# Second MLP product in three float32r products, interleaved tile by tile with the first

## The chip, the cores and the metric

The kernel runs on one core of a Trainium2 chip. The core has a matrix engine (TensorE, "PE" in the profile, with its weight loads as "PEld"), VectorE (DVE), ScalarE (ACT), GpSimd (POOL) and a queue engine SyncE (SP) that issues most of the DMA transfers. Each engine works off its own instructions in order, and they meet through semaphores. SBUF is the working memory of 128 partitions; PSUM holds TensorE's results in eight banks of 128 x 512 float32. The metric is device time in microseconds (us), the median of the runs. The profile is one more execution, with its own span, from its first to its last instruction.

## The reference

Two stages follow each other. The first is a state-space scan over 4 batches, 8 heads and 768 tokens, 32 channels and 16 states per head. It is computed in pieces of the sequence:

```python
cum = np.cumsum(log_a)                                   # within the piece
M = (C @ B.T) * exp(cum_i - cum_j) * causal
y = M @ x + (C @ state) * exp(cum)
state = exp(sum(log_a)) * state + sum_j exp(cum_end - cum_j) * B_j x_j
```

The second takes the scan's result as 3072 tokens of 256 features:

```python
h = x @ w_in                        # 256 -> 2048
g = h * clip(h + 3, 0, 6) / 6
out = g @ w_out                     # 2048 -> 256
```

The two weight arrays arrive as float64 words (8 bytes each) and are decoded to float32 on the chip.

## The kernel before

The sequence is cut into six blocks of 128 tokens. A block holds these tokens of all four batches, so 512 columns. For each block k the scan produces yT (features by tokens, two tiles of 128 x 512), the first product makes the hidden tile h for each of 16 groups f of 128 hidden units, an activation turns it into gT, and the second product sums over the 16 groups. The program is written in the order in which each engine runs it (a manual schedule); nothing reorders it.

*Head and block 0.* The scan of block 0 is done first. Then `mlp_in` runs the first product of block 0 in plain float32, while the weights, in eight pieces of 1 MB, are loaded into `raw` (three buffers) and decoded: `decode` is a generator of steps on ScalarE and VectorE (L206 to L254), and steps of the next pieces are woven between the groups of block 0. `split_w` splits each piece of `w_in` into a high part, a low part and a combination called gap. `first_out` (L735) is the second product of block 0, in float32 with the tokens as output rows, and is stored by two plain DMAs.

*Blocks 1 to 5, first product.* `lead` (L684 through `in_product`) multiplies the gap parts of weight and y, and the result is scaled in PSUM (L697 on VectorE or L700 on ScalarE). `follow` adds high times high and low times low on top. These three float32r products give the full float32 product. ScalarE (L707) and VectorE (L708) then make gT. Six PSUM banks rotate for h, and `lead` runs two groups ahead.

*Blocks 1 to 5, second product.* It starts when the block's gT is complete. It is one level of a Strassen-Winograd scheme in float32: seven products in place of eight, on quarters of gT and w_out. The sums of weights (`weight_sums`) are made once, the sums of gT (`g_sums`, L780) by GpSimd in each block. For blocks 1 to 4 `wide_units` (L861) keeps the output features on partitions and the tokens in columns; the result is transposed in 32 x 32 squares on VectorE (L875) and stored by 32 DMAs of 16 KB (L882). The last block uses `out_units` (L794): tokens on partitions, and four plain stores (L847).

*The scan of the next block* (`scores`, `multiply`, `mix`, `from_state`, `renew`: L548, L589, L615, L521, L560) is put between the products of `wide_units`, all eight heads at once. The decay factors are loaded as rows, masked by GpSimd (`conceal`, L162) and exponentiated by ScalarE, one call of 128 x 64 per batch and head with the column's own sum as bias (`decay`, L406, 32 calls per block). The loads of the coming blocks, `load_bc`, `load_x` and `rows`, are issued by SP in program order with the stores.

Of the kernel before, what the change touches and what calls it, by code (L numbers as in the profile page):

```python
# [21 lines left out]
def kernel(  # L22
# [12 lines left out]

    nc = tc.nc
# [22 lines left out]
    ffn = ctx.enter_context(tc.tile_pool(name="ffn", bufs=1))  # L70
    ps = ctx.enter_context(tc.tile_pool(name="ps", bufs=1, space=PSUM))
    ps_o = ctx.enter_context(tc.tile_pool(name="ps_o", bufs=2, space=PSUM))
    ps_y = ctx.enter_context(tc.tile_pool(name="ps_y", bufs=1, space=PSUM))
    dram = ctx.enter_context(tc.tile_pool(name="dram", bufs=1, space=DRAM))
    ctx.enter_context(tc.manual_schedule())


    pre = ffn.tile([P, NF, TB], FP32, name="pre", tag="gT")
    G = NB * NH


    moe_w_in, moe_w_out = moe_w_in.bitcast(U32), moe_w_out.bitcast(U32)
    a_sb = pre[:G, 0:2].rearrange("g t i -> g (t i)")[:, :S]
# [5 lines left out]
    def load_bc(c):  # L89


# [19 lines left out]
        Bs[c] = tokens_first(B, nc.scalar if c == 0 else nc.sync, name="B")  # L111
# [7 lines left out]
    def load_x(c):  # L119
# [4 lines left out]
    w_high, w_low, w_gap = (  # L124
        const.tile([P, NK, DF], FP32R, name=n) for n in ("w_high", "w_low", "w_gap"))
    w_out = const.tile([P, NF, DM], FP32, name="w_out")
# [4 lines left out]

    def load_w(i, queue=nc.sync):

# [12 lines left out]
    load_w(0, nc.scalar)  # L146
    load_bc(0)
    load_x(0)
    load_w(1)
    nc.scalar.preload_act_table_set("natural_log_exp_and_others")  # L150


# [16 lines left out]
    run = pre[:G, 2:4].rearrange("g t i -> g (t i)")[:, :S]  # L169
# [7 lines left out]
    half_up = const.tile([P, 1], FP32, name="half_up")  # L177
    nc.vector.memset(half_up, UP / 2)
# [14 lines left out]
    first_in = {}  # L193

    def decode(i):

# [33 lines left out]
        if i and i + NRAW < 2 * NP:  # L233
            load_w(i + NRAW)
# [3 lines left out]
        if i < NP:  # L238
            if i < 2:
                dst = ffn.tile([P, NK, FP * P], FP32, name="w32", tag=("wide", "back")[i])  # L240
                first_in[i] = [dst[:, j] for j in range(NK)]
                m, e = (t.rearrange("p (k f) -> p k f", k=NK) for t in (m, e))
            else:
                first_in[i] = [y_tile("w32", FP32) for j in range(NK)]
                for j, dst in enumerate(first_in[i]):
                    sl = slice(j * FP * P, (j + 1) * FP * P)
                    nc.vector.scalar_tensor_tensor(  # L247
                        out=dst, in0=m[:, sl], scalar=2.0 ** -20, in1=e[:, sl], op0=ALU.mult,
                        op1=ALU.mult)
                return  # L250
        else:
            dst = w_out[:, (i - NP) * FP:(i - NP + 1) * FP, :]
            m, e = (t.rearrange("p (k f) -> p k f", k=FP) for t in (m, e))
        nc.vector.scalar_tensor_tensor(  # L254
            out=dst, in0=m, scalar=2.0 ** -20, in1=e, op0=ALU.mult, op1=ALU.mult)

    pick = const.tile([P, G], BF16, name="pick")  # L260
    less = const.tile([P, G], BF16, name="less")
    picks = ffn.tile([P, G * N], BF16, name="picks", tag="u2")
    mid = pre[:G, 9].bitcast(BF16)[:, :2 * P]
    low = pre[:G, 10, :2 * P]

    cum = pre[:G, 4:6].rearrange("g t i -> g (t i)")[:, :S]
# [74 lines left out]
    def y_tile(name, dtype):  # L341
        return att.tile([P, TB], dtype, name=name, tag="y", bufs=6)

    yTs, states, mids, bTs, bss, tmps = {}, {}, {}, {}, {}, {}
    ys, cbs, sps, adds = {}, {}, {}, {}

    ds = {}

    def diff_mask(c, b):

        if c == 0:
            d = ps.tile([P, NH, HT], FP32, name="d", tag=f"f{b}")
        elif b < 2:
            d = ps_o.tile([P, NH, HT], FP32, name="d", tag="o")
        else:
            d = ps_y.tile([P, NH, HT], FP32, name="d", tag=f"y{b % 2}")
        nc.tensor.matmul(
            out=d, lhsT=ident_h, rhs=hide.unsqueeze(1).to_broadcast([P, NH, HT]),
            start=True, stop=True)
        ds[c, b] = d  # L360

    def mask_again(c, b):

        nc.tensor.matmul(
            out=ds[c, b], lhsT=ident_h, rhs=hide.unsqueeze(1).to_broadcast([P, NH, HT]),
            start=True, stop=True)
# [21 lines left out]
    def first_eto():  # L388

        e_ps = ps.tile([P, NB, HT], FP32, name="e_ps", tag="f0")  # L390
# [10 lines left out]

    def decay(c, b):

        for h in range(NH):
            g = b * NH + h
            nc.scalar.activation(  # L406
                Ls[c][:, b, h], Ls[c][:, b, h], AF.Exp, bias=cum_n[:, c, g:g + 1])
# [5 lines left out]

# [8 lines left out]

# [12 lines left out]
    def turn_ps(c, j):  # L435

        if c < 2:
            return ps.tile([P, NB, P], FP32, name="t_ps", tag=f"f{2 * j if c else 1}")
        return ps_o.tile([P, NB, P], FP32, name="t_ps", tag="o")

# [7 lines left out]
    def turn_b(c):  # L448

        t_ps = turn_ps(c, 1)  # L450
        transposes(c, 1, t_ps)
        nc.scalar.copy(out=turned(c)[0], in_=t_ps)

    def turn_c(c, t_ps):

        transposes(c, 0, t_ps)
# [10 lines left out]

        nc.vector.tensor_tensor(out=turned(c)[2], in0=t_ps, in1=etos[c], op=ALU.mult)

    def turn(c, j):  # L470
        if j:
            turn_b(c)
        else:
            t_ps = turn_ps(c, 0)
            turn_c(c, t_ps)
            fade_c(c, t_ps)

    def wake(c):
        from_start(c)
        carry(c)  # L480
        for b in range(NB):
            ends(c, b)

    def turn_squares(t, out):

# [15 lines left out]
    def turn_all(c):  # L501
        bT, _, csT = turned(c)
        for t, out_ in zip(bcs[c], (csT, bT)):
            turn_squares(t, out_)
        part_heads(c)
        fade(c)
# [636 lines left out]
```

## Time and profile before

| | us |
|---|---|
| runs | 362.24, 359.21, 362.02 |
| median | 362.02 |
| profiled execution, span | 356.9 |
| TensorE busy | 337.6 (95%) |
| VectorE busy | 223.0 (62%) |
| ScalarE busy | 183.1 (51%) |
| GpSimd busy | 165.1 (46%) |
| mean granted TensorE clock | 0.999 |

The profile states its execution's span, 356.9 us; what lies around the span is not in it, and the runs are 2.3 to 5.3 us above it. A busy share is the sum of an engine's instructions over the span. TensorE's instructions overlap, so the spacing of a run of matmuls says more than their duration. A float32 matmul appears as two records, a float32r matmul as one. A line such as "150.09 21.50 PE h L684 x92" of the chain of work reads: from 150.09 us on, for 21.50 us, 92 records of line 684 that write h. A window's line gives its bounds and length, then for PE, PEld, DVE, ACT and POOL the busy time and the number of records, then the granted clock, the DMA share and GB/s.

### The profile page before, as it was taken

How to read it: one execution, taken by the hardware profiler on the slowest of the kernel's cores; microseconds unless marked ns; L12 is line 12 of the kernel's file. 1: busy time of each engine (PE TensorE's matmuls, PEld its weight loads, DVE VectorE, ACT ScalarE, POOL GpSimd, SP SyncE). 2: the span in 40 equal slices, each digit the busy share in tenths (PEclk: the TensorE clock that was granted, in tenths of full speed). 3: DMA queues.
4: the chain of work that ended last, by engine and by line, in shares of the span. 5: the costliest groups of instructions: out<-in, count | busy, mean ns of one | idle time of the engine just before them, and what ended most of it. 6: DMA issues, size and time to landing. Idle time of an engine off the chain costs nothing.

```text
span 356.9 us, 8261 instructions
## 1 busy us (share of the span) xinstructions
PE 337.6 (95%) x3408; PEld 266.9 (75%) x3408; DVE 223.0 (62%) x341; ACT 183.1 (51%) x380; POOL 165.1 (46%) x155
## 2 busy tenths in 40 slices
PE   6999768899799999999999999999999989999996
PEld 2654225688687888888888887888888778888996
DVE  6689999976567654967345777327677313577011
ACT  3779678655876375166293266292466021466000
POOL 3304667075139981239931259911079600079600
PEclk9999999999999999999999999999999999999999
DMA  7989637800693007524106624106110001110000
GB/s 168 204 330 153 151 118 158 165 2 3 92 194 57 17 3 119 109 35 66 30 2 105 125 34 66 31 2 77 24 21 2 2 2 17 28 18 0 2 29 29
DMA packets 91604, 24.88 MB, mean 70 GB/s; under 512 B 84208, under 2 KB 87952, under 8 KB 91056
## 3 DMA queue, kind: packets, MB, share of 16 engines
q1 hardware_dynamic: 87184, 23.06, 33.3%
q10 hardware_dynamic: 4384, 1.31, 1.6%
q8 instruction: 26, 0.43, 0.5%
q14 instruction: 10, 0.08, 0.1%
HBM read 21.07 MB, written 3.29 MB: 68 GB/s over the span
## 4 chain that ended last, share of the span: by engine, by line
PE 77%; DVE 14%; ACT 3%; DMA 3%; issue 1%; SPq 1%; DVEq 0%
PE h L684 31%; PE wb L861 12%; PE wc L861 8%; PE wa L861 8%; PE o L735 4%; PE oa L794 4%; PE ob L794 4%; DVE gT L720 3%; PE y L615 2%; PE y L521 2%; DVE w L247 2%; PE cb L548 2%; DMA raw<-in_moe_w_in_dram 2%; ACT L L406 2%; DVE wse L225 2%
## 5 line engine op out<-in xcount | busy, mean ns | idle before, releaser
L708 DVE SCALAR_TENSOR_TENSOR gT<-gT,h 128x512 f32<-128x512 f32 x80 | 55.0, 688 | 33.5 <-ACT gT L707 30.5
L707 ACT ACTIVATE gT<-h,half_up 128x512 f32<-128x512 f32 x80 | 55.2, 690 | 36.2 <-PE h L684 36.2
L780 POOL TENSOR_TENSOR s<-gT 128x512 f32<-128x512 f32 x20 | 25.8, 1290 | 66.4 <-DVE gT L708 66.4
L684 PE MATMUL h<-gap,w_gap 128*128 128x512 f32 x160 | 51.7, 408 | 2.0 <-DVE gap L677 2.0
L684 PE MATMUL h<-high,w_high 128*128 128x512 f32 x160 | 50.7, 398 | 0.3 <-DVE h L697 0.3
L684 PE MATMUL h<-low,w_low 128*128 128x512 f32 x160 | 50.3, 395 | 0.0
L700 ACT ACTIVATE h<-h 128x512 f32<-128x512 f32 x40 | 23.6, 589 | 30.2 <-PE h L684 30.2
L684 PEld LDWEIGHTS h<-gap,w_gap 128*128 128x128 f32 x160 | 29.9, 188 | 9.2 <-ACT high L675 1.6
L684 PEld LDWEIGHTS h<-high,w_high 128*128 128x128 f32 x160 | 29.6, 188 | 8.6 <-DVE h L697 1.8
L684 PEld LDWEIGHTS h<-low,w_low 128*128 128x128 f32 x160 | 30.1, 188 | 7.3
L641 PE MATMUL h<-yT,w 128*128 128x512 f32 x64 | 29.3, 603 | 4.8 <-DVE w L247 2.4
L735 PE MATMUL o<-w_out,gT 128*128 128x256 f32 x128 | 29.0, 382 | 3.0 <-DVE w_out L254 3.0
L406 ACT ACTIVATE L<-L,cum_n 128x64 f32<-128x64 f32 x128 | 31.4, 337 | 0.0
L861 PE MATMUL wb<-s,w_out 128*128 128x256 f32 x128 | 30.7, 382 | 0.0
L589 DVE TENSOR_TENSOR L<-L,cb 128x512 f32<-128x512 f32 x24 | 15.3, 681 | 22.8 <-PE cb L548 19.7
L735 PEld LDWEIGHTS o<-w_out,gT 128*128 128x128 f32 x128 | 23.9, 190 | 7.4 <-ACT gT L715 2.3
L697 DVE TENSOR_SCALAR h<-h 128x512 f32<-128x512 f32 x40 | 27.7, 692 | 1.2 <-PE h L684 1.2
L641 PEld LDWEIGHTS h<-yT,w 128*128 128x128 f32 x64 | 11.6, 189 | 21.8 <-issue 10.4
L780 POOL TENSOR_TENSOR gT<-gT 128x512 f32<-128x512 f32 x20 | 26.7, 1337 | 0.0
L861 PEld LDWEIGHTS wb<-s,w_out 128*128 128x128 f32 x128 | 24.0, 190 | 3.5
L162 POOL TENSOR_SCALAR_AFFINE_SELECT L<-L 64x1024 f32<-64x1024 f32 (+1 forms) x16 | 18.6, 1166 | 17.3 <-DMA L<-cum_d 17.0
L780 POOL TENSOR_TENSOR s<-s,gT 128x512 f32<-128x512 f32 x20 | 25.7, 1287 | 1.6
(143 smaller groups left out, 558.4 us busy)
## 6 DMA issues: line engine op xcount, KB each, us to landing
raw<-in_moe_w_out_dram SPq DMA_DIRECT2D x4, 1024.0 KB
L<-cum_d SPq DMA_DIRECT2D x8, 512.0 KB
xt<-in_x_dram SPq DMA_DIRECT2D x6, 512.0 KB
raw<-in_moe_w_in_dram SPq DMA_DIRECT2D x3, 1024.0 KB
out_dram<-back SPq DMA_DIRECT2D x128, 16.0 KB
eto<-cum_e SPq DMA_DIRECT2D x20, 64.0 KB
B<-in_B_dram SPq DMA_DIRECT2D x5, 256.0 KB
raw<-in_moe_w_in_dram ACTq DMA_DIRECT2D x1, 1024.0 KB
```

The lines of the kernel that those rows point to most:

```text
L162: nc.gpsimd.affine_select(out=t[rows], in_=t[rows], pattern=pattern, compare_op=ALU.is_ge, fill=-1e5, base=base, channel_multiplier=-1)
L406: nc.scalar.activation(Ls[c][:, b, h], Ls[c][:, b, h], AF.Exp, bias=cum_n[:, c, g:g + 1])
L641: nc.tensor.matmul(out=h.rearrange("p r i -> p (r i)"), lhsT=first_in[f // FP][j][:, f % FP * P:(f % FP + 1) * P], rhs=yTs[k][j], start=(j ...
L684: nc.tensor.matmul(out=h, lhsT=w[:, j, f * P:(f + 1) * P], rhs=y[j], start=(start and j == 0), stop=True, skip_group_check=True)
L697: nc.vector.tensor_scalar(out=h, in0=h, scalar1=-Z / UP, scalar2=None, op0=ALU.mult)
L700: nc.scalar.mul(h, h, -Z / UP)
L707: nc.scalar.activation(g, h, AF.Relu, bias=half_up, scale=UP * UP / 6.0)
L708: nc.vector.scalar_tensor_tensor(out=g, in0=g, scalar=UP, in1=h, op0=ALU.min, op1=ALU.mult)
L735: nc.tensor.matmul(out=o[:, b % 2], lhsT=gTs[0][:, f, b * P:(b + 1) * P], rhs=w_out[:, f], start=(f == 0 and b % 2 == 0), stop=True, skip_ ...
L780: nc.gpsimd.tensor_tensor(out=o, in0=p_, in1=q_, op=op)
L794: nc.tensor.matmul(out=bank[:, slot], lhsT=lhs[:, j], rhs=rhs[:, j], start=(clear and j == 0), stop=True, skip_group_check=True)
L861: nc.tensor.matmul(out=bank[:, slot], lhsT=lhs[:, j], rhs=rhs[:, j], start=(clear and j == 0), stop=True, skip_group_check=True)
```

## The change

The second product of blocks 1 to 5 becomes three float32r products, as the first one is. `split_o` splits the pieces of `w_out`, and each activated tile g is split too: `g_high` on ScalarE, `g_low` on VectorE, `g_gap` on GpSimd. The Winograd sums go. The output features lie on partitions and the 512 tokens in columns for all six blocks, in two pairs of PSUM banks (A for high and low, G for gap). `gather` and `join` combine them, and `store` transposes and writes, for every block, the last one included. In the last block the last two groups are multiplied in float32 without a split.

The two products are interleaved: the tile of group f-3 is multiplied by `w_out` directly behind the first product of group f, and the last two groups of a block lie in the next block. h has two banks now, and all scales of `lead` run on ScalarE. The scan of the next block is spread over the groups by a plan of slots, in two rounds of four heads that share two banks ("xy"). In block 0 the second product runs in the same loop, and the scan of block 1 with it. The decay factors get their column sums on GpSimd (`add_cum`), and ScalarE takes the exponential in one call of 128 x 512 per batch.

```diff
-            nc.scalar.activation(
-                Ls[c][:, b, h], Ls[c][:, b, h], AF.Exp, bias=cum_n[:, c, g:g + 1])
+    def add_cum(c, b):
+        hs = slice(b * NH, (b + 1) * NH)
+        nc.gpsimd.tensor_tensor(
+            out=Ls[c][:, b], in0=Ls[c][:, b],
+            in1=cum_n[:, c, hs].unsqueeze(2).to_broadcast([P, NH, HT]), op=ALU.add)
+    def decay(c, b):
+        nc.scalar.activation(Ls[c][:, b], Ls[c][:, b], AF.Exp)
...
+    def g_high(k, f):
...
+        nc.scalar.mul(gs[k, f][1], g, CUT * Z)
+    def g_low(k, f):
+        g, high, low_, _ = gs[k, f]
+        nc.vector.scalar_tensor_tensor(
+            out=low_, in0=high, scalar=-1.0 / Z, in1=g, op0=ALU.mult, op1=ALU.add)
+    def g_gap(k, f):
+        _, high, low_, gap = gs[k, f]
+        nc.gpsimd.tensor_tensor(out=gap, in0=high, in1=low_, op=ALU.subtract)
+    def second(k, f):
...
+            product(accs[k][0][m], high_w[:, f % FP, cols], high_g, start=(f == 0))
+            product(accs[k][0][m], lows[NP + f // FP][:, f % FP, cols], low_g)
+            product(accs[k][1][m], gap_w[:, f % FP, cols], gap_g, start=(f == 0))
...
+    def store(k, m):
+        stage, back = staged()
+        nc.vector.transpose(out=back[:, m], in_=stage[:, m])
+        for t in range(4):
+            r0 = k * P + 32 * t
+            t0 = t // 2 * NB * HT + t % 2 * 32
+            for q in range(4):
+                c0 = m * P + 32 * q
+                nc.sync.dma_start(
+                    out=out.rearrange("(b s) m -> s b m", b=NB)[r0:r0 + 32, :, c0:c0 + 32],
+                    in_=back[32 * q:32 * q + 32, m].rearrange(
+                        "i (n m) -> i n m", m=32)[:, t0 // 32:t0 // 32 + 2 * NB - 1:2])
```

The loop of blocks 1 to 5 and the end, after the change (`go` runs what the plan has put into a slot of this group):

```python
            follow(k, f)
            lead(*more)                     # the next group
            ramp(k, f)
            scale(*more)
            go(t, "ramp")
            gate(k, f)
            go(t, "gate")
            g_high(k, f)
            go(t, "act")
            g_low(k, f)
            go(t, "low")
            go(t, "pool")
            g_gap(k, f)
            second(k, f - 3)                # for f < 2: second(k - 1, 14 + f)
            go(t, "pe")
...
    for m in range(2):
        gather(LAST, m)
    for m in range(2):
        for f in range(NF - 2, NF):
            second_whole(LAST, f, m)
        join(LAST, m)
        store(LAST, m)
```

## The prediction

> **What bounds the kernel now.** I read the page's busy shares first, then the chain that ended last in order of time, then the stage windows, the waits, and last the issuing queue.
>
> ```profile
> PE 337.6 (95%) x3408; PEld 266.9 (75%) x3408; DVE 223.0 (62%) x341; ACT 183.1 (51%) x380; POOL 165.1 (46%) x155
> ```
>
> TensorE is busy 95% of the span, so only its own work, its waits, or what lies before its first and behind its last matmul can move the end. The chain in order of time (start us, us, what) gives the price of a matmul in each mode:
>
> ```profile
> 150.09 21.50 PE h L684 x92
> ...
> 197.62 1.73 PE wb L861 x8
> ...
> 351.85 1.80 PE oa L794 x16
> 353.67 0.42 DVE res L838
> ```
>
> 92 float32r matmuls (512 columns) in 21.50 us are 0.2337 us each. A float32 matmul leaves two records: eight records of 256 columns take 1.73 us, 0.216 us each, so 0.43 us per 256-column instruction and 0.86 us per 512-column one (the two records of L641 also start 0.43 us apart). The chain cuts the 356.9 us into: 0 to 22.67 head; to 97.08 block 0; then 53.0, 51.9, 51.6, 53.5 and 46.6 us for blocks 1 to 5; and 3.3 us from the last matmul to the end. The timed median is 362.02, 5.1 us above the span (the runs: 2.3 to 5.3); I work on the span and add the same 5.1.
>
> Block 0 is another regime. The stage windows (length, then busy us per engine):
>
> ```profile
> 26.00:67.00 41.00, 33.19 (x90) 15.99 (x88) 40.69 (x45) 30.90 (x45) 21.81 (x14) 1.00 0.74 156
> ...
> 202.00:253.60 51.60, 51.60 (x530) 43.03 (x529) 30.26 (x50) 26.95 (x66) 25.16 (x24) 1.00 0.27 39
> ```
>
> From 26 to 67 VectorE is the bound (40.69 of 41.00, decoding the weights); in block 3 TensorE is never idle and VectorE, ScalarE and GpSimd have 21 to 26 us each to spare. Last, one store of the transposed output on its queue, with its durations (min/median/max ns), and a run of 32 of them:
>
> ```profile
> L882 SPq DMA_DIRECT2D out_dram<-back x128: 315/430/798, 143.1 to 315.4; - x128
> ```
>
> ```profile
> 197.60 16.87 SPq L882 DMA_DIRECT2D out_dram<-back  x32
> ```
>
> 32 stores keep SP 16.87 us, 0.53 us each. Today that lies under the next block's matmuls, and the last block doesn't use this path: it ends with four plain stores.
>
> **Matmuls, part by part.** (1) Second product, blocks 1 to 4: the Winograd form goes, 56 float32 instructions or 112 records, 112 x 0.2157 = 24.2 us; 96 float32r matmuls come, 96 x 0.2337 = 22.4 us. Gain 1.7 us per block; in the last block 112 instructions of 128 columns (25.1 us) become 84 float32r and 4 float32 of 512 columns, 19.6 + 3.4 = 23.0 us, gain 2 us. (2) The first product keeps 96 per block. (3) The scan's small matmuls stay: 0.55 + 0.98 + 0.79 + 1.41 + 0.62 = 4.35 us per block. So the sum of TensorE work is: head 22.67; block 0 60 x 0.86 + 0.47 (first lead) + 0.87 (transposes) + 4.35 = 57.3; block 1 (it takes over two tiles of block 0's second product in float32) 180 x 0.2337 + 3.4 + 4.35 + 0.87 = 50.7; blocks 2 to 4 192 x 0.2337 + 4.35 = 49.2 each; block 5 190 x 0.2337 + 3.4 = 47.8. Together the last matmul could end at 326.1, against 353.65 now; most of that distance is the wait and idle time of blocks 0 and 1.
>
> A page of the Trainium skill, TensorE: Matmul & The Clock Gate (Wait — 56ns, not 53.3ns?), gives back-to-back matmuls N columns at 2.4 GHz plus 2.5 ns, 215.7 ns at 512. The float32 records agree (216 ns), the float32r ones don't (233.7 ns at a granted clock of 1.00); by the page the 468 new float32r matmuls would be 8.4 us cheaper, but the row decides.
>
> **What of this waits.** Block 0: VectorE has after 27.3 us 6 pieces to decode at 4.65 us without disturbance (0.42 + 0.43 + 0.68 + 1.21 + 0.68 + 1.23, the rows of the pieces decoded at 67 and later), 16 gates at 0.675, three weight splits at 1.23, and the scan, now drawn in here, some 8.3 (four products at 0.68, state updates 2.0, y parts 2.9, fade 0.69): 27.9 + 10.8 + 3.7 + 8.3 = 50.7 us. In the window above four pieces took 29.5 us beside the gates, 10.9 more than 4 x 4.65, while GpSimd was busy 21.8 us; the change gives GpSimd about as much there (three splits of 1024 columns at 3.1, masks 4.7, sums 4 x 1.29, row ends and carry 3.6), so again +11: 27.3 + 61.7 = 89, and 3.5 us of second product stand behind the last piece. Block 0 ends at 92 (86 to 98), 12 us above its matmuls.
>
> Block 1: five more splits. GpSimd: 16 x 1.29 to 1.5 (the new gap tiles) + 5 x 3.1 + masks 4.7 + cum sums 6.5 + the rest 3.9 = 51 to 55 us; VectorE: 16 x (0.69 + 0.69 to 1.0) + splits 6.2 to 11 + scan 8.3 + 7.6 = 44 to 54. Both reach TensorE's 50.7. The second product follows three tiles behind, about 4 us of slack; I take 55.2 (51 to 60).
>
> Blocks 2 to 4: per tile TensorE needs 12 x 0.2337 = 2.80 us. ScalarE: ramp 0.69, scale 0.59, high part 0.63, so 30.6 per block, + four wide exponentials 2.4 + 3.4 = 36; the wide form replaces 32 calls (0.337 us each, 0.25 apart), off the path in these blocks (in block 0 they stood on it for 5.6 us, which the forecast's 92 holds already). VectorE 37 to 42, GpSimd 33 to 37. All below 49.2, so TensorE bounds, but h has two banks only: after the high and low products of one tile, ramp and scale (1.28 us and two handovers, about 1.5) must be done before the next tile's, with 1.87 us of other matmuls in between. At the third tile of each block nothing of the second product stands there and 1 us is lost; where two of the scan's vector operations fall into one tile I allow 1 more. 51.2 each (49.7 to 54); block 5, without scan, 49. The queues moved past: SP issues the loads of the next block's rows (6.9 us at 190.5) and of B and C (11.2 us at 214.5), then the two stores (17 us), then x, some 36 us into the block's 49; x is first needed in the next block, some 18 us later, so I cost this at nothing; were it late, TensorE would stand for as long.
>
> **The end.** Now the last block too is joined, transposed and stored through 2 x 16 small stores on SP. The first half's join and transpose (0.69 + 0.71) lie beside the other half's 1.73 us of matmuls, so SP starts about when the last matmul ends. The 17 stores started from 307.6 to 315.4, with nothing else on the queue, are 0.49 us apart, those above 0.53: the 32nd issue starts 15.2 to 16.4 us later. From the last issue's start to the end the trace shows 2.8 us (354.1 to 356.9). The end comes 18.0 to 19.2 us behind the last matmul, less 0.2 for SP's early start; I take 18.4, against 3.3. Nothing lies beside it: this is the term that decides.
>
> Sum: 92 + 55.2 + 3 x 51.2 + 49 + 18.4 = 368.2, that is 11.3 above 356.9, or 362.0 + 11.3 = **373 us**.
>
> **Rivals.** (a) *TensorE is never held up* (12 in 100): with all waits gone the end is 326.1 + 18.4 = 344.5, so 349.6 us timed: faster. It decides the sign: I add 23.7 us of waits (12 in block 0, 4.5, 3 x 2 and 1.2 in the others), break-even is at 12.4. Block 0 alone decides it; if VectorE's 11 us of disturbance there go (less GpSimd work at the same moment), the sum is 357, no change. For it: the work is spread over tiles. Against it: VectorE's full window.
>
> (b) *VectorE becomes the bound* (20 in 100). In this trace L254's 1024 columns take 1225 ns where GpSimd rests and up to 2183 where it works, and L247's 512 columns 1.7 us instead of 0.69. The new low part has two inputs in SBUF as well and GpSimd is busy two thirds of blocks 2 to 4. If each low part waits for half a GpSimd operation, 0.65 us more, VectorE needs 16 x 2.03 + 8.3 + 6.8 = 47.6 of 49.2 and in scan tiles more than TensorE: some 3 us more per block, 4 x 3 = 12, 385 us. Against it: the gap tile follows its own low part, and the next low part comes 2.8 us later; L677 (two inputs in SBUF) has median 693, maximum 993. The Trainium skill, SBUF — State Buffer (Who interferes with whom), says that such a VectorE instruction and a GpSimd one that reads SBUF lock each other out for a whole instruction; the rows of L254 agree, those of L677 mostly don't.
>
> (c) *The stores are issued faster in the quiet end* (8 in 100): at the minimum, 0.315 us and 0.04 between two, the 32nd starts 11.0 us after the first and the end comes 4.7 us earlier, 368.6. It isn't likely, as the 17 stores with SP to themselves took the median of 0.43 nearly all. The remaining 60 are for the forecast.
>
> **Numbers.** Bounds: block 0 -6/+6, block 1 -4/+5, blocks 2 to 4 -4.5/+8, the end -4.5/+1; not all at one end, so about -10/+10 round 373, and the upper one drawn out to (b)'s 385. Range 361 to 385, leaving out most of (a). A difference of 1% (3.6 us) is about what a measurement tells from none. Faster by over 1%: 0.09 (most of a); within 1%: 0.11 (the rest of a, and the best ends of the forecast); slower: 0.80.
>
> **What would show it.** The chain of after ends with some 15 us of issuing and landing behind the last matmul; block 0 ends between 86 and 98 with VectorE full; the first to the last matmul of blocks 2 to 4 take 50 to 54 us each; the 468 new matmuls are 0.234 us apart. The prediction is wrong if the stores are issued well under 0.4 us each, if block 0 ends before 82, or if ramp and scale hold up every tile, not one (then over 390).

## The result: 400.7 us, 11% slower, and the profile after

The changed kernel takes 400.72 us (median of 4 runs, 398.06 to 402.35), the kernel before 360.62 beside it (358.67 to 362.24): a ratio of 1.109, 95% interval 1.102 to 1.116. The prediction said 373 (361 to 385) and slower. The direction was right, the size was not: 27.7 us are missing. The profiled execution took 400.51 us, its span is 398.8. In experiments 2 and 11 one run each (368.01 and 364.79 us) was in the kernel's slower state; the ranges and medians there hold it, the ratios do not.

First the page of the changed kernel: the busy shares, and the granted TensorE clock in 40 slices of 9.97 us.

```profile
PE 349.5 (88%) x3148; PEld 248.0 (62%) x3148; DVE 252.9 (63%) x366; ACT 219.7 (55%) x359; POOL 182.6 (46%) x161
...
PEclk9788999989999998999999989999999999999975
```

TensorE's share fell from 95% to 88%, no other engine took its place as the bound, and the clock row, all nines before, now has slices of 7 and 8. (The 7 and 5 at the end lie behind the last matmul and cost nothing.) The chain of work shows which steps held. Its rows in block 5 and at the end (start us, us, what):

```profile
349.37 1.40 PE h L656 x6
352.15 1.40 PE h L656 x6
354.93 1.40 PE h L656 x6
378.05 3.45 PE Aacc L656 x8
```

Two tiles of 12 float32r matmuls each take 5.56 us, 0.232 us a matmul: the price of the prediction, in the new product as well. The last matmul ends at 381.5, and the timeline of the issuing queue shows the last block's stores:

```profile
381.34 15.34 SPq L764 DMA_DIRECT2D out_dram<-back  x32
```

32 stores, 0.48 us each, and the end 17.3 us behind the last matmul, where 18.4 was forecast. The places in between, each from the first high product of one block to that of the next:

| | forecast us | measured us | difference |
|---|---|---|---|
| head, to the first matmul of the first product | 22.67 | 23.94 | +1.3 |
| block 0 | 69.3 | 75.6 | +6.3 |
| block 1 | 55.2 | 66.0 | +10.8 |
| blocks 2, 3, 4 | 51.2 each | 55.5, 56.6, 55.1 | +13.7 |
| block 5, to the last matmul | 49 | 48.7 | -0.3 |
| the end | 18.4 | 17.3 | -1.1 |
| span | 368.2 | 398.8 | +30.6 |

So the blocks with a scan in them carry the miss. Three things stand out in them: the scan's own matmuls, the stands of TensorE, and a half clock behind some stands.

*The scan.* The timeline of TensorE in the kernel before, where the next block's scan stands in block 3 (start us, us, what; the spacing of the starts is what counts): state products, scores, state updates, and then the product goes on.

```profile
228.21 0.61 PE L521 MATMUL y<-csT,state 32*64 32x64 f32 x25
...
228.70 1.18 PE L548 MATMUL cb<-cT,bT 32*64 32x128 f32 x61
229.81 0.86 PE L560 MATMUL y<-xt,bs 64*32 64x64 f32 x64
230.60 1.56 PE L861 MATMUL wb<-gT,t 128*128 128x256 f32 x6
```

The same view of the changed kernel, the scan in block 2; only the scan's rows are shown:

```profile
168.40 1.10 PE L471 MATMUL cb<-cT,bT 32*64 32x128 f32 x32
...
174.22 0.86 PE L482 MATMUL yy<-xt,bs 64*32 64x64 f32 x64 [0.35 <-PE h L656]
175.00 0.68 PE L460 MATMUL yy<-csT,state 32*64 32x64 f32 x16
175.61 0.86 PE L530 MATMUL yy<-L,xt 64*32 64x64 f32 x64
...
181.26 0.68 PE L460 MATMUL yy<-csT,mid 32*64 32x64 f32 x16 [0.53 <-ACT gh L706]
...
190.40 1.10 PE L471 MATMUL cb<-cT,bT 32*64 32x128 f32 x32
...
198.12 0.68 PE L460 MATMUL yy<-csT,state 32*64 32x64 f32 x16
198.73 0.86 PE L530 MATMUL yy<-L,xt 64*32 64x64 f32 x64
199.51 0.68 PE L460 MATMUL yy<-csT,mid 32*64 32x64 f32 x16
```

There are as many matmuls as before, but 16 state products now take 0.61 us (175.00 to 175.61), where 32 from four row tiles (the 32-row places in TensorE that `tile_position` gives a small matmul) stood between 228.21 and 228.70 (the rows left out mix the last seven of them with the first scores), and the groups stand apart. By start spacing, a block's four groups take 1.07 (state), 1.15 (scores), 1.41 (mix) and 0.79 us (update) before, 4.4 together, and 2.44, 2.06, 1.57 and 0.78 after, 6.9 together.

*The stands.* The waits of TensorE in the changed kernel (what waited, for whom, us in total, times, longest):

```profile
PE h L656 <- DVE g L696: 6.5, 4, 3.2
PE Aacc L656 <- DVE full L231: 6.0, 2, 4.2
PE yy L530 <- issue: 2.7, 2, 1.5
PE t_ps L403 <- DMA B<-in_B_dram: 2.6, 1, 2.6
PE h L656 <- ACT h L664: 2.3, 2, 1.5
```

In the timeline, block 0 has 10.7 us of stands, block 1 7.1, blocks 2 to 4 2.6, 2.3 and 2.4, block 5 0.9: 26.0 in all, against 23.7 in the forecast. The stands are not where the 30 us went.

*The half clock.* Three windows of 3.41 us, one behind the other, around the stand of 1.24 us in block 3's scan (window and length, then busy us and records of PE, PEld, DVE, ACT, POOL, then granted clock, DMA share, GB/s):

```profile
230.42:233.83 3.41, 2.17 (x105) 1.68 (x88) 1.89 (x3) 1.29 (x3) 1.16 (x2) 1.00 0.02 5
233.83:237.24 3.41, 3.41 (x10) 2.67 (x9) 1.01 (x3) 1.92 (x4) 0.23 (x1) 0.50 0.00 0
237.24:240.65 3.41, 3.41 (x29) 2.60 (x28) 1.00 (x4) 1.00 (x3) 1.28 (x1) 1.00 0.02 5
```

In the middle window TensorE has no gap, but a clock of 0.50. A busy share alone would not show it; it does half the work. After the head this happens five times (from 35.86, 80.23, 117.77, 148.49 and 233.83 us on), and 1.7 us of clock are lost each time, 8.5 in all; once more, for 6.83 us, in the head. The kernel before has stands too (9.8 us in block 0, none there over 1.54), and its profiled execution has no such stretch. Other executions of it have: in 37 that ran beside the experiments the mean clock is 0.986 to 1.000, and those at 0.999 or 1.000 took 358.8 to 359.4 us, those at 0.991 362.0 to 363.9. So lost clock goes with lost time in a program that is the same each time.

### The profile page after: what moved, and what is told of

The parts are those of the page before. It is cut to its first block, busy times and chain, and to the rows that moved or that the text cites. A ratio compares the mean times of both kernels' runs of the same rounds, so it can differ in the third digit from the quotient of the medians.

```text
span 398.8 us, 8035 instructions
## 1 busy us (share of the span) xinstructions
PE 349.5 (88%) x3148; PEld 248.0 (62%) x3148; DVE 252.9 (63%) x366; ACT 219.7 (55%) x359; POOL 182.6 (46%) x161
## 4 chain that ended last, share of the span: by engine, by line
PE 72%; DVE 9%; ACT 4%; issue 4%; DMA 3%; SPq 3%; POOL 1%; DVEq 0%; ACTq 0%
PE h L656 26%; PE Aacc L656 22%; PE Gacc L656 8%; PE h L644 5%; PE yy L460 3%; PE cb L471 2%; DMA B<-in_B_dram 2%; PE yy L530 2%; SPq L90 2%; ACT g L691 1%; DVE g L696 1%; PE yy L482 1%; ACT gh L706 1%; DMA pairs<-in_C_dram 1%; DVE state L492 1%
## 5 line engine op out<-in xcount | busy, mean ns | idle before, releaser
L715 POOL TENSOR_TENSOR gg<-gh,gl 128x512 fp32r<-128x512 f32 x78 | 102.5, 1314 | 114.4 <-DVE gl L710 98.9
L696 DVE SCALAR_TENSOR_TENSOR g<-g,h 128x512 f32<-128x512 f32 x78 | 53.1, 681 | 60.4 <-ACT g L691 59.8
L691 ACT ACTIVATE g<-h,ramp_bias 128x512 f32<-128x512 f32 x78 | 53.5, 686 | 65.3 <-PE h L656 64.2
L710 DVE SCALAR_TENSOR_TENSOR gl<-gh,g 128x512 fp32r<-128x512 f32 x78 | 59.3, 760 | 38.3 <-ACT gh L706 34.0
L656 PE MATMUL Aacc<-gh,oparts 128*128 128x512 f32 x156 | 62.4, 400 | 0.0
L656 PE MATMUL Gacc<-gg,oparts 128*128 128x512 f32 x156 | 62.2, 399 | 0.0
L656 PE MATMUL Aacc<-gl,low 128*128 128x512 f32 x156 | 61.9, 396 | 0.0
L656 PE MATMUL h<-yp,w_gap 128*128 128x512 f32 x160 | 52.4, 409 | 6.5 <-DVE g L696 6.5
L656 PE MATMUL h<-yp,w_high 128*128 128x512 f32 x160 | 54.4, 421 | 2.4 <-ACT h L664 2.3
L656 PE MATMUL h<-yp,low 128*128 128x512 f32 x160 | 51.0, 400 | 1.0 <-issue 1.0
L664 ACT ACTIVATE h<-h 128x512 f32<-128x512 f32 x80 | 47.2, 590 | 0.1
```

The lines of the kernel that those rows point to most:

```text
L656: nc.tensor.matmul(out=out_, lhsT=w, rhs=y, start=start, stop=True, skip_group_check=True)
L664: nc.scalar.mul(hs[k, f], hs[k, f], -1.0 / UP)
L691: nc.scalar.activation(g, hs[k, f], AF.Relu, bias=ramp_bias, scale=UP * UP / 6.0 / Z)
L696: nc.vector.scalar_tensor_tensor(out=g, in0=g, scalar=UP / Z, in1=hs.pop((k, f)), op0=ALU.min, op1=ALU.mult)
L710: nc.vector.scalar_tensor_tensor(out=low_, in0=high, scalar=-1.0 / Z, in1=g, op0=ALU.mult, op1=ALU.add)
L715: nc.gpsimd.tensor_tensor(out=gap, in0=high, in1=low_, op=ALU.subtract)
```

## The experiments

All times are medians. The ratios are against runs of the kernel before on the same chip, whose medians there are 359.4 to 362.3 us. "After" is the changed kernel, 400.72 us.

**1. The end: stores on two queues.**

```diff
-                nc.sync.dma_start(
+                queue = nc.scalar if k == LAST and q % 2 else nc.sync
+                queue.dma_start(
```

> The changed kernel, but the last block's 32 stores are issued alternately by SP and ScalarE, which has nothing left to do there. Theory: the end is bound by the issue of one queue (17.3 us from the last matmul to the end, 32 issues 0.5 us apart). Then 16 issues per queue take 8 us and the end shrinks to about 9.5 us: 392.5 to 393.5 us timed against 400.7. Rival: what makes the descriptors, or the writing of 128-byte pieces, is shared and sets the rate; then the issues of each queue get slower and the time stays within 2 us of 400.7.

Measured: 392.12 us (389.85 to 393.15), ratio 1.084 [1.078, 1.090]. The two queues in its timeline:

```profile
380.66 7.45 SPq L765 DMA_DIRECT2D out_dram<-back  x16
```

```profile
380.66 7.63 ACTq L765 DMA_DIRECT2D out_dram<-back  x16
```

Both queues issue at the same time, each 16 stores at 0.47 us, and 8.6 us are gone, 7.6 of them at the end (9.7 us behind the last matmul in place of 17.3). So the end is the issuing and not the transfer, and the price is per queue. The Trainium skill, DMA: Bandwidth & Descriptors (Issuing engines are not separate DMA queues), says that starting transfers from several engines saves only the sequencer's time, "usually small relative to the DMA itself". What was saved agrees with that; for stores of 16 KB behind the last matmul it was not small.

**2. The scan: only the order of its rounds, in the kernel before.** Scores and state products of pairs 0 and 1 go first, then those of pairs 2 and 3, in the same place; nothing else.

```diff
-        for b in range(NB):
-            for a, rows in enumerate(HALF):
-                for q in range(NQ):
+        for some in ((0, 1), (2, 3)) if c else (range(NQ),):
+            for b in range(NB):
+                for a, rows in enumerate(HALF):
+                    for q in some:
```

> The kernel before with one edit: the score products and the products with the state of blocks 1 to 5 are issued for the head pairs 0 and 1 first, then for 2 and 3, in place of all four pairs in turn. Theory: in the changed kernel the small matmuls of the scan cost TensorE 6.9 us per block in place of 4.4, because two rounds of two pairs leave only two of the four row groups of the array to work at the same time. Then the records of these two lines take 3.2 to 4.5 us per block in place of 2.2, and the kernel gets 5 x 1 to 2.3 = 5 to 11 us slower: 366 to 372 us. Rival: they cost more in the changed kernel because they stand between the 512-column matmuls, with a changeover of some 0.2 us each; then the order alone does nothing: 360 to 362 us.

Measured: 364.14 us (361.79 to 368.01), ratio 1.008 [1.004, 1.011]. In block 2 the state products take 1.61 us and the scores 1.43 (1.07 and 1.15 before): 0.82 us a block from the order alone, a third of the 2.5. That is below what the theory expected, and the time lies between its range and the rival's.

**3. The scan: its rounds apart, in the kernel before.** In blocks 2 to 5 the scores of two pairs stand one product tile from those of the other two, and the state products and mixes go by two pairs as well. The second product keeps its seven float32 products.

```diff
-                    scores(c)
+                    scores(c, ((0, 1),))
+                if i == 3:
+                    scores(c, ((2, 3),))
```

> The kernel before with, in blocks 2 to 5, its scores in two pieces of two pairs placed one tile apart, and its state products and mixes by two pairs as well; the second product is untouched. Theory (the scan's extra TensorE time comes from the rounds standing apart, since four row tiles no longer run beside each other and each piece pays its own changeover): the four groups of small matmuls take 6 to 6.9 us in a block instead of 4.4, and the time is 366 to 369. Rival (only the order of the pairs counts, and the rest of the extra time in the changed kernel comes from the new product around it): 5.2 us in a block and about 364.

Measured: 376.03 us (372.66 to 376.68), ratio 1.036 [1.030, 1.043]. In one block (214.5 to 268.5 us) the groups take 2.17 + 2.02 + 1.57 + 0.86 = 6.6 us, in the theory's range: the new product around the scan is not needed for it. The time is 7 to 10 us above the range, and the waits tell why:

```profile
PE wc L871 <- DVE L L596: 5.8, 4, 1.5
```

The scores' banks, held longer now, keep a product waiting for 1.45 us in each of four blocks. The spans of the two profiled executions add up: 374.8 - 356.9 = 17.9, and 4 x 2.2 for the groups, 5.8 for the stands and 3.4 of lost clock are 18.0. (The medians are only 14.2 us apart: on that chip the kernel before lost clock too, 0.986 to 0.995.) The lost clock is the second find here. Four stands of the same 1.45 us, and two of them have a half clock behind them. Three of the 3.41 us windows that hold them:

```profile
187.44:190.85 3.41, 1.96 (x82) 1.58 (x73) 2.14 (x5) 2.22 (x10) 0.41 (x1) 1.00 0.02 5
242.05:245.46 3.41, 1.97 (x108) 1.66 (x103) 1.34 (x4) 1.38 (x6) 0.41 (x1) 1.00 0.02 5
300.06:303.47 3.41, 1.96 (x92) 1.60 (x84) 1.80 (x4) 0.37 (x1) 0.00 (x0) 1.00 0.02 5
```

TensorE is busy equally long in all three. The half clock follows only the second: it holds small matmuls alone (108 records), while the first holds four large ones behind the stand and the third three. The window of the fourth stand, 129.40 to 132.81 us, holds small ones alone too (112 records, 2.12 us busy), and a half clock follows it.

**4. The scan: its matmuls twice, in after.** Every small matmul of the scans of blocks 3 to 5 is issued twice, so these blocks' sums are not the reference's.

```diff
-        for b in range(NB):
+        for b in list(range(NB)) * (1 if c < 3 else 2):
```

> The changed kernel with each small matmul group of the scans of blocks 3 to 5 issued twice in its place (same operands; the sums hold the products twice, so the numbers of these blocks are not those of the reference, and no other work changes). It measures how much of a group's 6.9 us in a block is paid per matmul and how much per piece. Theory (a piece has a fixed cost of its own, so pieces that stand apart cost more; the matmuls themselves run at the rates seen when the two rounds stood next to each other, 1.61 + 1.43 + 1.5 + 0.79 = 5.3 us): TensorE's time in these groups goes from 6.9 to about 12.2 us per block, the whole to 400.7 + 3 x 5.3 = about 416.5. Rival (two row tiles beside each other are simply half as fast as four, per matmul): to 13.8 us per block and 421. Third (the matmuls run at the rates of the kernel before, and all of the rest is per piece): to 11.3 us per block and 414.

Measured: 416.60 us (414.48 to 417.81), ratio 1.157 [1.153, 1.162]. The time is that of the theory; the rival's 421 lies above the runs and the third's 414 just below the lowest. TensorE's time in the groups comes out between theory and rival: in block 3 4.36 + 3.80 + 3.03 + 1.41 = 12.6 us (7.0 in after), in block 2 13.3. Twice the matmuls take 5.6 to 6.4 us more, so of some 7 us about one is paid per piece and about 6 per matmul. The state products are the dearest: 64 more take 1.9 us, 0.03 us each, where 64 from four row tiles took 1.07 in the kernel before.

What stays untested is the obvious repair, rounds by batch in after (two batches, all eight heads), so that all four row tiles take turns in each round. A form of it was written, and 388 to 394 us were expected of it if it gave the 2.5 us a block back, 398 to 402 if not; that form could not be built, so there is no time for it.

**5. The stands: filled.** Eleven matmuls whose results nobody reads are put into the head and into block 0, where TensorE stands.

```diff
+    busy(2, bank("d", [NB * P], "G0"))
     scan_first()
...
+            if f2 == 8:
+                busy(4, bank("d", [NB * P], "G0"))
             second(0, f2)
+        if f == 3:
+            busy(3, bank("d", [NB * P], "G0"))
...
+    busy(2, bank("d", [NB * P], "G0"))
     second(0, 12)
```

> The changed kernel with 11 idle matmuls (0.86 us each, into a bank not in use) put where TensorE stands in the head and in block 0: 2 before the first scores, 3 where it waits for B of block 1, 4 and 2 where it waits for decoded pieces of w_out. Theory: in the changed kernel the granted clock falls to half for 3.5 to 7 us after each stand of more than 1 us (15 to 22, 36 to 40, 80 to 84 us), which costs TensorE 3.5 + 1.7 + 1.7 us; with the stands filled the clock stays at 1.00 up to block 1, and the kernel gets 3 to 6 us faster, 395 to 398 us. Rival: the clock falls for another reason, or VectorE bounds these places anyway; then the time is within 1.5 us of 400.7 or above, by as much as the idle matmuls delay.

Measured: 397.06 us (396.51 to 399.75), ratio 1.100 [1.095, 1.105]. The wait for decoded weights does not go away, matmuls now lie in it. The clock lost before the last matmul falls from 11.9 us to 1.7, and in the head and in block 0, where the matmuls were put, no half clock is left: it follows the stands. What it costs can't be read from the 3.7 us. The head is 1.0 us shorter. Block 0 is as long as before, 75.9 us: B's load lands 1.6 us later there, and behind the decoded piece a stand of 0.99 us for VectorE has come. The rest lies in blocks 1, 3 and 4, where no matmul was put; two half clocks of after (148.49 and 233.83 us) did not come there, though the stands before them did.

**6. Block 0: without the masks beside the decoding.** The timeline of GpSimd in after, and that of VectorE at the same time:

```profile
74.84 7.04 POOL L156 TENSOR_SCALAR_AFFINE_SELECT L<-L 64x1024 f32<-64x1024 f32 x4
```

```profile
74.01 1.96 DVE L201 SCALAR_TENSOR_TENSOR wm<-raw,wm 128x1024 f32<-128x1024 uint32 x1
75.89 1.62 DVE L225 TENSOR_TENSOR wse<-wse 128x1024 uint16<-128x1024 uint16 x1
77.55 2.05 DVE L231 SCALAR_TENSOR_TENSOR full<-wm,wse 128x1024 f32<-128x1024 f32 x1
```

Together with the three steps behind them (1.36, 1.24 and 1.52 us, the first ones of the last piece), the six steps take 9.75 us in place of 4.65. The run leaves out the masking of block 2's factors (`conceal`), which a causal product needs.

```diff
-        at(t, "pool", conceal, c, 0)
-        at(t + 1, "pool", conceal, c, 1)
+        if c > 2:
+            at(t, "pool", conceal, c, 0)
+            at(t + 1, "pool", conceal, c, 1)
```

> The changed kernel without the four mask operations of GpSimd for block 2's factors, which lie at 74.8 to 81.9 us in block 0 (the factors of block 2 are then not causal; that part of the computation is left out). Theory: VectorE's six decoding steps in that time take 9.75 us in place of 4.65 because GpSimd runs beside them, and TensorE stands 4.2 us for the decoded piece and then runs 3.7 us at half clock. Without the masks the stand falls to below 1 us and block 0 ends 4 to 6 us earlier: 395 to 397 us. Rival: VectorE's steps are slow for another reason, or the time comes back at the next wait (1.8 us, for the last piece): within 1.5 us of 400.7.

Measured: 397.49 us (395.38 to 399.59), ratio 1.100 [1.093, 1.106]: just above the theory's range, and the interval overlaps that of after, so the trace decides. The six steps take 6.3 us. The longest stand for decoded weights is 3.3 us in place of 4.2, where below 1 was expected, the half clock at 80 us is gone, and block 0 takes 73.2 us in place of 75.6. Of these 2.4 us, 0.7 come from the stand, which ends earlier, and 1.7 from the clock.

**7. Block 0: B and C loaded earlier.** The prediction has no term for the 2.6 us wait for B's load. Here the load of block 1's B and C is issued ahead of the third piece of weights.

```diff
+    load_bc(1)
...
-    load_bc(1)
```

> The changed kernel with the loads of B and C of block 1 issued before the third weight piece, at about 17 us in place of 27 us. Theory: TensorE stands 2.6 us at 33 to 35.6 us because the turn of B, which the change has drawn into block 0, waits for a load that lands 8.4 us after its issue, and half clock follows for 3.7 us (1.7 us lost). With the earlier load the stand goes: 2.5 to 4.5 us less, 396 to 398 us. Rival: the weight pieces come later by as much, and VectorE, which sets block 0, starts its decoding later: 399 to 403 us.

Measured: 399.62 us (398.84 to 401.56), ratio 1.107 [1.101, 1.112], no gain. The waits show where the stand went:

```profile
PE h L644 <- DVE g L652: 4.3, 4, 1.7
```

The wait for B is gone; the one for g, 1.7 us in after, is 4.3, and block 0 takes 76.2 us. Leaving the wait out made no error in the time, for a reason that the prediction did not give: in block 0 another chain is as late.

**8. Block 1: the split on VectorE.** All eight low and gap subtractions go from GpSimd to VectorE.

```diff
-        nc.gpsimd.tensor_tensor(out=gap, in0=hi_, in1=lo_, op=ALU.subtract)
+        nc.vector.tensor_tensor(out=gap, in0=hi_, in1=lo_, op=ALU.subtract)
...
-        nc.gpsimd.tensor_tensor(out=lo_, in0=w, in1=hi_, op=ALU.subtract)
+        nc.vector.tensor_tensor(out=lo_, in0=w, in1=hi_, op=ALU.subtract)
```

> The changed kernel, with the last step of the weight splits (8 subtractions of 1024 columns, five of them in block 1) on VectorE in place of GpSimd. Theory: what holds up block 1 (7.1 us without a matmul, 4.1 us of clock) is that VectorE instructions with two inputs in SBUF wait while GpSimd runs its long subtractions: the low part that follows the second split takes 2.88 us in place of 0.69, the split itself 2.04 in place of 1.22. VectorE then gets 8 x 1.22 us more work, but loses these waits; block 1 gets 4 to 7 us shorter and the kernel 394 to 398 us. Rival: VectorE is simply full there (44 to 54 us of work were worked out for 50.7); then 6 us more work for it make block 1 longer, 402 to 408 us.

Measured: 402.12 us (400.30 to 403.06), ratio 1.114 [1.107, 1.120]. Block 1 fell from 66.0 to 62.3, but block 0 ends 5.6 us later: its two stands for pieces decoded by VectorE have grown from 6.0 us to 8.2. Hence the next run.

**9. Block 1 alone.** The same, only for the subtractions that fall in block 1. There are five of them, two for the gap of `w_in` and three for the low part of `w_out`; the expectation speaks of four.

```diff
-        nc.gpsimd.tensor_tensor(out=gap, in0=hi_, in1=lo_, op=ALU.subtract)
+        (nc.vector if i >= 2 else nc.gpsimd).tensor_tensor(
+            out=gap, in0=hi_, in1=lo_, op=ALU.subtract)
...
-        nc.gpsimd.tensor_tensor(out=lo_, in0=w, in1=hi_, op=ALU.subtract)
+        (nc.vector if i >= 1 else nc.gpsimd).tensor_tensor(
+            out=lo_, in0=w, in1=hi_, op=ALU.subtract)
```

> The changed kernel with the third step of the split (the subtraction that gives the low part) on VectorE only for the four weight pieces whose step falls in block 1; block 0 stays as it is. Theory (block 1's length comes from GpSimd's subtractions standing beside VectorE's matmul evictions, so TensorE waits for g at the third tile and then runs at half clock): block 1 shrinks by 3 to 4 us as it did when all subtractions moved, block 0 keeps its 76 us, the time is 396 to 398. Rival (block 1's gain in that run came only because block 0 had become longer and left less to do): within 1.5 us of 400.7.

Measured: 397.98 us (395.20 to 399.09), ratio 1.098 [1.091, 1.105]; its interval overlaps that of after, so here the trace decides. Block 1 takes 62.1 us in place of 66.0. VectorE's timeline in after, and GpSimd's beside it:

```profile
110.14 2.04 DVE L633 SCALAR_TENSOR_TENSOR oparts<-oparts,full 128x1024 fp32r<-128x1024 f32 x1
112.11 2.88 DVE L710 SCALAR_TENSOR_TENSOR gl<-gh,g 128x512 fp32r<-128x512 f32 x1
...
116.83 0.67 DVE L696 SCALAR_TENSOR_TENSOR g<-g,h 128x512 f32<-128x512 f32 x1
```

```profile
111.06 3.38 POOL L636 TENSOR_TENSOR low<-full,oparts 128x1024 fp32r<-128x1024 f32 x1
```

And VectorE's in this run:

```profile
113.14 0.68 DVE L712 SCALAR_TENSOR_TENSOR gl<-gh,g 128x512 fp32r<-128x512 f32 x1
113.74 1.21 DVE L637 TENSOR_TENSOR low<-full,oparts 128x1024 fp32r<-128x1024 f32 x1
```

The low part g that took 2.88 us beside GpSimd's subtraction takes 0.68, and the subtraction 1.21 in place of 3.38. TensorE's stand there is 1.69 us in place of 3.23, and block 1 has no half clock (3.4 us lost in after). But the clock lost in the whole run is 11.9 us as in after: three stretches of after are gone and three others came, two in block 0 (one of them behind a stand of 1.91 us) and one behind 1.79 us in block 4. So block 0 is 2.2 us longer, and part of the 4 us is given back. The last of the stretches in block 0 (98.16 us) also shows the price of a half clock with nothing else around it: from the last stand to the end of block 0 the same matmuls take 4.83 us in place of 3.14.

**10. Three at once.** The two queues, the eleven matmuls and the late pieces on VectorE.

> The changed kernel with three of the edits at once: the last block's stores on two queues (8.6 us shorter alone), eleven idle matmuls in the stands of the head and of block 0 (3.7 shorter alone), and the low parts of block 1's pieces on VectorE (3 to 4 expected alone). Theory (three separate places, whose costs add up): 384 to 387, with under 2 us of clock lost before the last matmul. Rival (they draw on the same slack): 389 or more. Either way it stays above the kernel before by 6 per cent or more, since the second product's additional matmul time and the scan's are untouched.

Measured: 384.60 us (383.10 to 386.28), ratio 1.061 [1.054, 1.069]. 400.7 - 8.6 - 3.7 - 2.7 is 385.7: the three add up to within 1.1 us. The clock lost is 3.4 us, not under 2. It stays 22.7 us above the kernel before.

**11. The wide exponentials alone, in the kernel before.**

```diff
-                Ls[c][:, b, h], Ls[c][:, b, h], AF.Exp, bias=cum_n[:, c, g:g + 1])
+        nc.scalar.activation(Ls[c][:, b], Ls[c][:, b], AF.Exp)
```

> The kernel before with the wide exponentials alone: GpSimd adds the column sums behind its masks, ScalarE takes 4 exponentials of 128x512 per block in place of 32 of 128x64. Theory: the narrow ones stand on the chain for 5.6 us at the end of block 0 only (84.6 to 90.5), there 23 calls become 4 and the kernel gets 2 to 4 us faster, 357 to 359 us; elsewhere nothing. Rival: GpSimd's sums (1.04 us each in the changed kernel) come later than what they replace, or its sums for the Winograd form are pushed back and hold up the second product: 361 to 364 us.

Measured: 361.00 us (358.45 to 364.79) against 362.34, ratio 0.996 [0.993, 1.000]: in the rival's range and not the theory's, and too small a difference to tell from none.

## Why the prediction was right in direction and wrong in size

*The end* (18.4, measured 17.3), the step that "decides", held, and experiment 1 shows its cause. Rival (c) did not come: the issues are 0.48 us apart. *The price of a float32r matmul* (0.2337 us) held, and with it block 5 (49, measured 48.7), where there is no scan.

*"The scan's small matmuls stay: ... 4.35 us per block"* failed: 6.9. This is the largest term, 5 x 2.5 = 12.5 us. I counted instructions and took their price from a kernel where four row tiles run beside each other and the groups lie together. Two rounds change both; experiments 2, 3 and 4 show it, in both kernels. That the 12.5 us come back when the rounds are undone in after is not shown.

*A wait was costed at its own length.* The stands were sized well in sum (23.7, measured 26.0), in block 0 by luck: 2.6 us there are the wait for B's load, which has no term in the prediction (block 0 10.7 of 12, block 1 7.1 of 4.5, blocks 2 to 4 7.3 of 6, block 5 0.9 of 1.2). What failed is the silent step that TensorE goes on at full clock behind a stand: 8.5 us of clock after the head were lost that way. Experiment 5 shows that filling the stands gives the clock back, though in block 0 not the time; experiments 6 and 9 show the 1.7 us in one stretch each. The profile before could not warn: its clock row is whole.

*Block 1* (55.2, bounds 51 to 60, measured 66.0): some 2.5 of the 10.8 us are the scan, 2.6 more stands, 3.4 half clock; 2.3 are in the spacing of the large matmuls. Moving the subtractions off GpSimd (experiment 9) takes 3.9 us away in all: the half clock goes, and the stands fall from 7.1 us to 5.9. So rival (b) was right about the mechanism, in one place. In blocks 2 to 4 it wasn't: the low parts have a median of 692 ns and a mean of 738, 0.05 us over in place of its 0.65.

*Block 0* ended 7.5 us later than the 92 (86 to 98). By TensorE's time that is 1.3 from the head, 2.5 scan, 3.4 half clock and 1.7 in the spacing of the large matmuls; the stands were 1.3 us shorter than allowed. But the 92 was reached by VectorE's work, 61.7 us from 27.3 on without a wait, and that step failed too. The window from 27.3 us to the end of TensorE's last wait for a decoded piece, and VectorE's waits in it:

```profile
27.30:96.40 69.10, 58.37 (x436) 28.00 (x435) 54.15 (x71) 39.27 (x50) 22.48 (x16) 0.95 0.63 121
```

```profile
DVE g L652 <- ACT g L651: 14.4, 9, 4.9
```

VectorE is busy 54 us, less than forecast, and stands 14.4 us for the next g, which comes from TensorE's product. The two engines wait for each other in turn; neither is full. So a repair on one side alone comes back in part on the other, as in experiments 5 and 7.

*Blocks 2 to 4* (51.2, bounds to 54, measured 55.1 to 56.6): besides the 2.5 of the scan, the 192 large matmuls of block 2 take 46.1 us without the stands, 0.240 us each, where the price is 0.2337: 1.2 us more, and 0.7 and 0.8 in blocks 3 and 4 (half clock taken off). It comes from the changes between large and small matmuls, five groups of small ones in each block: the large one before a group and the first behind it stand 0.33 to 0.34 us from the next, where others stand 0.23. I had priced none.

The terms together, scan 12.5, half clock 8.5, stands 2.3, spacing of the large matmuls 6.7 (1.7 and 2.3 in blocks 0 and 1, 2.7 in blocks 2 to 4), head 1.3, end -1.1, make 30.2 of the 30.6 us. This is an account of TensorE's time, not a sum of what repairs would give. In blocks 0 and 1 the spacing was not traced further. Against it, what lies around the span was set at 5.1 us and is 1.7 (400.51 - 398.8), so the timed miss is 3 us smaller.

"If ramp and scale hold up every tile (then over 390)" is not what put the time over 390: TensorE waits for the scale in L664 for 2.3 us in all. Rival (a), no stands at all, did not come either; with the scan's 12.5 us more its span of 344.5 would have been 357, no change.

One reading in the prediction is wrong, without weight in the sum: the float32 records of 216 ns (L861) have 256 columns, so they don't agree with a price of 215.7 ns for 512; float32 records of 512 columns (L641) start 430 ns apart.

## What to carry to other kernels

Price a matmul by the group it stands in: the same small matmuls in two rounds, with large ones between them, took 6.9 us in place of 4.4. Price a stand of TensorE with what follows it: read the granted clock in windows of some 3.4 us, not the busy share. Where a stand can't go, filling it can keep the clock, but gains time only if no other wait takes it back. And ask of every change that trades a plain end for many small transfers how long its queue takes to issue them when nothing is left to hide it.

## What the runs showed that was not expected

The half clock comes in steps of 3.41 us. In after its stretches begin at 15.38, 35.86, 80.23, 117.77, 148.49 and 233.83 us; the distances are 6, 13, 11, 9 and 25 times 3.413 within 0.02 us, and each lasts 3.41 us or, in the head, 6.83. In experiment 9 the five stretches lie on such a grid too, with another beginning. The Trainium skill, TensorE: Matmul & The Clock Gate (What's actually happening), describes a free-running window of 3413 ns in which activity is measured; the traces agree. It also gives a rule for practice (Why this matters for your kernels), no gaps over about 3 us between matmuls, and there the measurement decides otherwise: a window that held a stand of 1.92 us was followed by half clock, and one with 1.24 us and many small matmuls too. The two closest cases with large matmuls alone, in after:

```profile
93.88:97.30 3.42, 1.61 (x5) 0.68 (x4) 2.43 (x4) 1.30 (x3) 0.09 (x1) 1.00 0.89 179
145.08:148.49 3.41, 1.49 (x7) 1.13 (x7) 2.65 (x4) 1.31 (x3) 2.42 (x3) 1.00 0.00 0
```

The first (TensorE busy 1.61 of 3.42 us) keeps its clock, the second (1.49 of 3.41) loses it. That a busy share just under half is the limit, and that small matmuls count for less, is read from the stands of four traces; no run was made for it, and experiment 11 has a case against a sharp limit (92.03 to 95.44 us, eight records of large matmuls, 1.83 us busy, half clock behind it). Where a stand falls in the grid decides as well: the stand of 1.9 us in block 1, at 147 us in after, has a half clock behind it there and in experiment 6, and none in experiments 5 and 7.

In the scans of blocks 2 to 4 TensorE also stands three times, for 1.0 to 1.5 us, at "issue", where the trace names no releaser. With the scan's matmuls doubled the stands moved (behind the 82nd of 128 mixes, or the 8th state product), but did not grow with them: 1.4 at most. The packets of the DMA queues point to the cause. The one packet that moved around the stand of 1.24 us (230.0 to 233.5 us in after) is of a queue that the page calls instruction:

```profile
q8 instruction: 1, 0.02, 1.7%
```

All 38 stands of TensorE at "issue" of over 0.3 us in the thirteen traces end 1.2 to 1.6 us after such a packet of 16 KB has landed. So TensorE most likely waits there for its next instructions. Most of the 24 such packets of after have no stand behind them, and no run was made for it.
